# Attention values paired per head pair, converting loads of q and k, and output sums added by transfers: a fused attention and two-FFN kernel on one core

## The chip, the cores and the metric

The kernel runs on one core of one Trainium2 chip. A core has a matrix engine (TensorE, PE in the profile; its weight loads are PEld), three other compute engines (VectorE DVE, ScalarE ACT, GpSimd POOL) and a sync engine (SP). Each engine works through its own instruction list in order and waits on semaphores. Transfers are issued from the lists of SP, ACT and POOL and are carried by 16 DMA engines. The metric is device time in microseconds (us): the kernel before takes 1067.9 us, the median of three runs (1066.99, 1067.9 and 1069.63).

## The reference, cut to what matters

```
# attention: 4 batches, 8 heads, 576 positions, 64 columns a head
scores = (q @ k.T) / sqrt(64);  bias = -(cum_i - cum_j), cum = cumsum(relu(s))
p = softmax(where(causal, -1e9, scores + min(bias, 0)))     # divided by sum + 1e-9
x = p @ v                                                    # to 2304 tokens x 512
# first FFN, 512 -> 2048 -> 512
h = x @ w_in;  g = h if h >= 1, 0 if h <= -1, else (h + 1)^2 / 4;  y1 = g @ w_out
# second FFN, 512 -> 1536 -> 512
y2 = ((y1 @ w_a) * (y1 @ w_b)) @ w_out2
```

## The kernel before, in words

Everything is kept transposed, features on partitions and tokens along the free dimension. A batch has 576 tokens, which the FFN products take in two halves of 288 columns. For accuracy most products are split: a value is stored as a high word rounded to the format fp32r and a low word that holds the rest, and three products (high x high, high x low, low x high) are summed in PSUM. Products of plain fp32 operands need no split.

**Attention.** Query positions are cut in five tiles of 116 rows (the last has 112). For the 8 heads of batch 0 (QK32 = 8) the scores are plain fp32 products (line 644) on the raw q and k with the bias as extra rows. For batches 1 to 3 the scores (line 653) are two fp32r products on a tile `qk` of four planes: planes 0 and 1 hold the high words of q and k on both partition halves, planes 2 and 3 hold the high word of q again and the low words. `load_head` brings q and k into `qkraw` twice (four transfers from SP), ScalarE or GpSimd rounds them into `qk` (`qkhi`, `q1`, lines 374 and 378) and VectorE makes the low words (`qklo`, line 614). There are two `qkraw` and two `qk` tiles, so a head's load waits for the scores of the head two before it. VectorE adds the mask and takes the row maximum (line 672), ScalarE exponentiates (line 687), TensorE transposes the probabilities (line 712), and ScalarE, or VectorE in batch 0, copies them to SBUF as `pt`.

**Values.** `values` multiplies `pt` with v for one head and one of two regions of query columns (0 to 231, 232 to 575). A head has only 64 columns of v, half the array, so a region is cut at MID (146 and 430): its left piece is computed by the left 64 array columns and its right piece by the right 64, with the same v as weights. PV32 = 32 means that all 32 heads take this fp32 form. Two copies by ScalarE put the two pieces in place in `xraw`, which holds a pair of heads. The pair is scaled by the reciprocal sums (over PE in batch 0, over a round trip through DRAM in the other batches) and split in two words.

**FFN.** Batches 0 and 1 use plain split products (line 981). Batches 2 and 3 use a form of Strassen's method with seven products instead of eight for the first product of each layer (line 1128), with prepared forms of activations and weights. `y_step` makes the second product of a layer for a group of 3, 4 or 8 feature tiles: the first group is copied from PSUM to a tile y (ScalarE), each later one is added to it by VectorE (line 1223), and in layer 2 the finished tile is sent to the output by SP.

**Order.** The order on every engine is not the order of the code. A planner in the kernel (`Plan.run`) holds all operations with a key (a due time) and estimated costs, and places them engine by engine: of the first 24 in key order that have their buffers it takes the one that can start first. The keys come from the table ATT (start, end of each batch's attention), ENDS, LEAD (how long before use weights are fetched), AHEAD and OFFSET (within the seven products), and POOL_UNTIL (until which key GpSimd may take casts). On the chip an instruction waits for its semaphores only; the keys fix nothing but the order in each list.

Of the kernel before, what the change touches and what calls it, by code (L numbers as in the profile page):

```python
# [10 lines left out]
F32 = mybir.dt.float32  # L11
# [6 lines left out]
P = 128  # L18
# [8 lines left out]
ATT = ((0, 10, 60, False), (1, 65, 97, False), (2, 165, 350, True), (3, 340, 500, True))  # L27
# [8 lines left out]
ENDS = 1050  # L36
POOL_UNTIL = 100


OFFSET = (0.0, 0.15, 0.3, 0.45, 0.8, 0.95, 1.1)  # L40
AHEAD = 10
QK32 = 8
PV32 = 32
# [246 lines left out]
def tile_forgetting_attention_two_ffn(  # L290
# [35 lines left out]
    MID = (146, 430)  # L326
    REG_ALL = [len(j) * w for j, w in zip(REG_J, REG_W)]
    NG2 = NC // 2
    PE1 = 0.000456
    PE4 = 0.00168  # L330

# [77 lines left out]
    vs_room = room("vs", 1, [P, NQ, 2, D], F32R, "att")  # L409
# [4 lines left out]
    pt_rooms = [room(f"pt{g}_", 2, [QT, n], F32R, "att") for g, n in enumerate(REG_ALL)]  # L414
# [3 lines left out]
    hs_room = room("hs", 1, [P, S - PVSPLIT], F32, "att")  # L418
# [167 lines left out]
    def load_head(b, h, key):  # L586
# [14 lines left out]
        for u in range(2):  # L601
            for w in range(2):
                dma(key, lambda u=u, w=w: raw.t[u * D : (u + 1) * D, w], lambda w=w: qk[bh, :, w], D * S * 4, (),
                    [(raw, (u, w))], "qk", issue=0.6)
# [3 lines left out]
        op(casts(2 * S, key), key + 1,  # L608
           lambda e: copy(e, t.t[:, 0:2], raw.t), [(raw, (u, w)) for u in range(2) for w in range(2)],
           [(t, "hi"), (t, "lo")], name="qkhi")  # L610
        op(casts(S, key), key + 1, lambda e: copy(e, t.t[D:, 2], raw.t[D:, 0]), [(raw, (1, 0))] + ones_set, [(t, "q1")], name="q1")

# [3 lines left out]
           [(raw, (1, 0)), (raw, (1, 1)), (t, "hi")], [(t, "lo")], name="qklo", port=True)  # L616
        load_v(b, h, st, key)

    def load_v(b, h, st, key):
        vr = st["v"] = Ref(v_room, key)  # L620
        dma(key + 0.5, lambda: vr.t, lambda: v[b * H + h], P * NQ * D * 4, (), [(vr, 0)], "v")
        if b * H + h >= PV32:
            vs = st["vs"] = Ref(vs_room, key)
            op(casts(NQ * D, key), key + 1, lambda e: copy(e, vs.t[:, :, 0], vr.t), [(vr, 0)], [(vs, 0)], name="vhi")
            op({DVE: tt(NQ * D)}, key + 1,
               lambda e: nc.vector.tensor_tensor(vs.t[:, :, 1], vr.t, f32(vs.t[:, :, 0]), op=ALU.subtract),
               [(vr, 0), (vs, 0)], [(vs, 1)], name="vlo", port=True)

    def scores(b, h, i, key):
# [31 lines left out]
        need = [(t, j) for j in ("hi", "lo", "q1", ("bias", 0), ("bias", 1))] + ones_set  # L661
# [31 lines left out]
    def transposes(b, h, i, key):  # L693
# [7 lines left out]
        def part(t, kr, js):  # L701
            return t[:kr, js[0] * w : (js[-1] + 1) * w].rearrange(
                "k (j q) -> k j q", q=w
            )[:, :, q0 : q0 + r]

        for j0 in range(0, i + 1, 4):
# [12 lines left out]
            hi = st["pt"][0][g]  # L719
# [9 lines left out]
            if b * H + h >= PV32:  # L729
                lo = st["pt"][1][g]  # L730
                op({DVE: tt(n)}, key,
                   lambda e, src=src, js=js, kr=kr, lo=lo: nc.vector.tensor_tensor(
                       part(lo.t, kr, js), src(), f32(part(hi.t, kr, js)), op=ALU.subtract),
                   [(pt, 0), (hi, (i, j0))], [(lo, (i, j0))], name="ptlo")

    def values(b, h, g, key):
        st = heads[b, h]
        e = h % 2
        x = st["x"]
        a0, b0 = e * D, (1 - e) * D  # L740
# [3 lines left out]
        pts = [t[g] for t in st["pt"]]  # L744
        vt = st["v"] if b * H + h < PV32 else st["vs"]
        w = hi - lo
        need = [(t, (i, j0)) for t in pts for i in range(NQ) if (QT * i >= PVSPLIT) == (g == 1) for j0 in range(0, i + 1, 4)]
        need += [(vt, 0)] if b * H + h < PV32 else [(vt, 0), (vt, 1)]
        if b * H + h < PV32:


            mid = MID[g]
            ends = ((0, lo, mid), (D, mid, hi))

            def mm2(_):
                for j in js:
                    o = j * REG_W[g] - lo
                    for c0, l, u in ends:
                        q0 = max(l, QT * j)
                        if q0 >= u:  # L760
                            continue
                        nc.tensor.matmul(  # L762
                            ps.t[c0 : c0 + D, q0 - l : u - l],
                            vt.t[: rows[j], j],
                            pts[0].t[: rows[j], o + q0 : o + u],
                            start=(j == 0),
                            stop=(QT * (j + 1) >= u),
                        )

            cols = max(sum(max(0, u - max(l, QT * j)) for j in js) for _, l, u in ends)  # L770
            op({PE: cols * PE4 + 0.15}, key, mm2, need, [(ps, 0)], hold=[x], name="pv")
            for n, (c0, l, u) in enumerate(ends):
                op({ACT: act(u - l)}, key + 0.001 * n,
                   lambda e, c0=c0, l=l, u=u: copy(e, x.t[a0 : a0 + D, l:u], ps.t[c0 : c0 + D, : u - l]),
                   [(ps, 0)], [(x, (h % 2, g, n))], name="pvx")
            return
# [571 lines left out]
```

## Time and profile before

| what | value |
|---|---|
| median of three runs | 1067.9 us (1066.99 to 1069.63) |
| span of the profiled execution, first to last instruction | 1066.3 us |
| TensorE busy | 1047.7 us, 98% of the span |
| VectorE, ScalarE, GpSimd busy | 748.9, 612.8, 43.7 us |
| mean granted TensorE clock | 0.993 |
| transfers | 152.34 MB, mean 143 GB/s |

The time of the profiled execution is told by its span; the median of the runs is 1.6 us longer than that span. A time in a view counts from the span's start. "Busy" is the time in which an engine had at least one instruction under way. TensorE's matmuls overlap, so the time that one of them takes out of the engine's list is read from the difference of two starts, not from its own duration.

### The profile page before, as it was taken

The page shows a single profiled execution, that of the slowest core. Times are in us where ns is not written, and L with a number is a line of the kernel's source. Part 1 is how long each engine was busy: PE and PEld are TensorE (multiplying, and loading weights), DVE is VectorE, ACT ScalarE, POOL GpSimd, SP SyncE. Part 2 cuts the span into 40 slices and gives each one's busy share as a digit, 9 for nine tenths or more (in the row PEclk, how much of TensorE's full clock was granted, in tenths as well). Part 3 has the DMA queues.
Part 4 walks back from the last instruction along what each step waited for, and adds up shares of the span by engine and source line. Part 5 has one row for each costly group of instructions (what it writes and reads, how often), then busy time and mean ns, then how long its engine had stood idle before and what let it go on. Part 6 is the DMA issues. An engine that isn't in the chain of part 4 may idle for free.

```text
span 1066.3 us, 20668 instructions
## 1 busy us (share of the span) xinstructions
PE 1047.7 (98%) x8080; PEld 1003.4 (94%) x8080; DVE 748.9 (70%) x1471; ACT 612.8 (57%) x1332; POOL 43.7 (4%) x69
## 2 busy tenths in 40 slices
PE   9989998999999999999999999999999999999998
PEld 5769988999999999989999999999999999999998
DVE  6889867377787786657856677838576887378473
ACT  5878885666777876865775343645536543332130
POOL 2122320000000000000000000000000000000000
PEclk9999998999999999999999999999999999999999
DMA  5466639564564455545624464431313332231102
GB/s 174 158 209 201 210 118 276 185 224 143 176 215 157 149 198 188 183 139 163 209 87 147 168 229 173 150 101 58 119 40 120 96 103 80 80 99 61 41 1 89
DMA packets 71041, 152.34 MB, mean 143 GB/s; under 512 B 7592, under 2 KB 32168, under 8 KB 70944
## 3 DMA queue, kind: packets, MB, share of 16 engines
q1 hardware_dynamic: 70848, 150.88, 43.0%
q8 instruction: 63, 1.03, 0.4%
q14 instruction: 34, 0.28, 0.1%
q10 hardware_dynamic: 96, 0.15, 0.0%
HBM read 107.64 MB, written 42.79 MB: 141 GB/s over the span
## 4 chain that ended last, share of the span: by engine, by line
PE 92%; ACT 2%; DMA 2%; DVE 1%; issue 1%; SPq 1%; POOL 1%; ACTq 0%; DVEq 0%; POOLq 0%
PE pp L981 53%; PE pp L1128 12%; PE ps L1128 9%; PE ps L762 5%; PE ps L712 4%; PE ps L981 4%; PE ps L653 2%; PE ps L644 1%; PE pp L653 1%; DMA qkraw<-in_qk 1%; PE pp L644 1%; SPq L386 1%; DMA set<-keep_in 1%; ACT qk L374 1%; DMA conv<-in_w_in 1%
## 5 line engine op out<-in xcount | busy, mean ns | idle before, releaser
L981 PE MATMUL pp<-g,whl 128*128 128x288 f32 x2376 | 327.5, 296 | 0.0
L981 PEld LDWEIGHTS pp<-g,whl 128*128 128x128 f32 x2376 | 319.6, 189 | 0.8
L981 PE MATMUL pp<-x,whl 128*128 128x288 f32 x1896 | 270.4, 299 | 0.8 <-DVE early L1017 0.7
L981 PEld LDWEIGHTS pp<-x,whl 128*128 128x128 f32 x1896 | 256.9, 190 | 3.5 <-DVE early L1017 1.3
L1128 PE MATMUL pp<-form,set 128*128 128x288 f32 x960 | 149.0, 298 | 1.5 <-DVE ct L1147 1.5
L1128 PEld LDWEIGHTS pp<-form,set 128*128 128x128 f32 x960 | 133.6, 188 | 3.1 <-DVE ct L1147 2.0
L1128 PE MATMUL ps<-form,set 128*128 128x288 f32 x720 | 113.4, 296 | 0.7 <-DVE form L1099 0.7
L1223 DVE TENSOR_TENSOR y<-pp,y 128x576 f32<-128x576 f32 x76 | 57.4, 756 | 67.1 <-PE pp L981 66.7
L1128 PEld LDWEIGHTS ps<-form,set 128*128 128x128 f32 x720 | 101.6, 188 | 0.9 <-DVE form L1099 0.9
L687 ACT ACTIVATE p<-p,mx 112x576 f32<-112x576 f32 (+4 forms) x140 | 81.5, 583 | 7.5 <-DVE mx L672 6.6
L374 ACT COPY pt<-ps 112x112 f32<-112x112 f32 (+4 forms) x172 | 64.1, 391 | 21.1 <-PE ps L712 17.7
L1147 DVE TENSOR_TENSOR ct<-ps,ct 128x288 f32<-128x288 f32 x80 | 36.4, 455 | 51.5 <-PE ps L1128 39.4
L672 DVE CUSTOM_DVE_ANT_0 p<-ps,hide 116x116 f32<-116x116 f32 (+1 forms) x112 | 49.9, 453 | 29.2 <-PE ps L653 23.5
L942 ACT ACTIVATE conv<-conv 128x512 uint32<-128x512 uint32 x68 | 45.9, 675 | 41.5 <-DVE conv L952 28.0
L712 PE MATMUL ps<-ident,p 116*116 116x116 f32 (+2 forms) x420 | 62.5, 265 | 2.5 <-ACT pt L374 2.0
L762 PEld LDWEIGHTS ps<-pt,v 116*64 116x64 f32 (+1 forms) x832 | 51.4, 136 | 14.3 <-issue 7.8
L962 DVE TENSOR_TENSOR whl<-conv,whl 128x512 fp32r<-128x512 f32 x68 | 47.0, 697 | 25.3 <-ACT whl L374 24.6
L762 PE MATMUL ps<-pt,v 116*64 116x146 f32 (+5 forms) x832 | 62.6, 285 | 0.5 <-ACT pt L374 0.4
L374 ACT CAST whl<-conv 128x512 fp32r<-128x512 f32 x58 | 35.5, 617 | 38.5 <-PE pp L981 37.3
L712 PEld LDWEIGHTS ps<-ident,p 116*116 116x116 f32 (+2 forms) x420 | 46.0, 135 | 8.6 <-ACT pt L374 3.0
L1169 ACT CAST g<-ct 128x576 fp32r<-128x576 f32 x56 | 36.7, 675 | 29.3 <-PE pp L981 17.5
L653 PE MATMUL ps<-qk 128*116 128x116 f32 (+1 forms) x192 | 46.7, 337 | 5.8 <-DVE qk L614 4.0
(112 smaller groups left out, 1325.4 us busy)
## 6 DMA issues: line engine op xcount, KB each, us to landing
whl<-keep_out SPq DMA_DIRECT2D x36, 512.0 KB
qkraw<-in_qk SPq DMA_DIRECT2D x112, 144.0 KB
conv<-in_w_out SPq DMA_DIRECT2D x28, 512.0 KB
keep_out<-whl SPq DMA_DIRECT2D x28, 512.0 KB
conv<-in_w_in SPq DMA_DIRECT2D x16, 512.0 KB
keep_in<-whl SPq DMA_DIRECT2D x16, 512.0 KB
conv<-in_w_a SPq DMA_DIRECT2D x12, 512.0 KB
conv<-in_w_b SPq DMA_DIRECT2D x12, 512.0 KB
```

The lines of the kernel that those rows point to most:

```text
L374: nc.scalar.copy(o, i)
L653: nc.tensor.matmul(pv()[:r, a, :w], t.t[:, 2 * u, QT * i : n], t.t[:, 2 * u + 1, a * w : (a + 1) * w], start=(u == 0), stop=(u == 1),)
L672: nc.vector.tensor_tensor_reduce(out=psl(pref.t)[:r].rearrange("q (g n) -> q g n", g=parts), in0=pv()[:r, :parts, :w], in1=hide[:r, lag : ...
L687: nc.scalar.activation(p, p, AF.Exp, bias=mx.t[:r], scale=-1.0, accum_out=sm.t[:r, h % 2, i : i + 1])
L712: nc.tensor.transpose(pt.t[: rows[j], (j - j0) * QT : (j - j0) * QT + r], psl(pref.t)[:r, QT * j : QT * j + rows[j]], ident[:r, :r],)
L762: nc.tensor.matmul(ps.t[c0 : c0 + D, q0 - l : u - l], vt.t[: rows[j], j], pts[0].t[: rows[j], o + q0 : o + u], start=(j == 0), stop=(QT * ...
L942: op({ACT: act(512)}, k, lambda e: nc.scalar.activation(up(), low(), AF.Copy, scale=2.0**-29), [(wide, 0)], [(we, 0)], name="wlow")
L962: op({DVE: tt(512)}, k + 1, lambda e: vec.tensor_tensor(half(1), value(), f32(half(0)), op=ALU.subtract), [(wr, 0), (hl, 0)], [(hl, 1)], n ...
L981: nc.tensor.matmul(bank_of(ps, a)[:, :HN], w(wu), x(xu)[:, a * HN : (a + 1) * HN], start=(k == 0 and t == 0), stop=(k == len(terms) - 1 an ...
L1128: nc.tensor.matmul(at(to), by_pair(st.t)[:, w, wu, g], forms[b, layer, g].t[:, x, xu], start=fresh and k == 0, stop=k == len(terms) - 1, s ...
L1169: op({ACT: act(S)}, k, lambda e, f=f: nc.scalar.copy(g[f].t[:, 0], t.t[:, f]), need[f], [(g[f], 0)], name="ghi")
L1223: nc.vector.tensor_tensor(o, i, o, op=ALU.add)
```

## The change: what it does

1. **Values of a head pair.** `values` now works on two heads at once: the even head's product goes to the left 64 array columns and the odd head's to the right 64, over the whole region. It runs after the odd head's probabilities. One copy moves the whole 128-partition result to `xraw`. The cut MID and the split form are gone; `pt` needs less room, since the fifth key tile has only 112 query columns.
2. **High words by converting transfers.** `load_head` of batches 1 to 3 issues five transfers from GpSimd's list that read q and k from DRAM and write rounded words straight to `qk`: four for planes 0 and 1 on both halves (`qkhi`), one for the second copy of q (`q1`). The casts on ScalarE and GpSimd go. SP still loads q and k once to the upper half of `qkraw` for the low words.
3. **Layer 2's output sums by adding transfers.** Every group of layer 2 is copied from PSUM to y by ScalarE or VectorE. The first group goes to the output by SP; each later one by a transfer from GpSimd's list that adds to what is in DRAM. There are 40 adding transfers. Layer 1 is as before.
4. **New keys.** ATT, ENDS, LEAD, POOL_UNTIL, OFFSET and AHEAD have new values, which with the new costs gives a new order on all engines.

```diff
-ATT = ((0, 10, 60, False), (1, 65, 97, False), (2, 165, 350, True), (3, 340, 500, True))
+ATT = ((0, 12.083, 59.239, False), (1, 54.172, 107.501, False), (2, 110.043, 361.002, True), (3, 337.937, 539.099, True))
...
+PV2 = 0.00143
...
 # load_head, batches 1 to 3
-        for u in range(2):
-            for w in range(2):
-                dma(key, lambda u=u, w=w: raw.t[u * D : (u + 1) * D, w], lambda w=w: qk[bh, :, w], ...
+        for w in range(2):
+            dma(key, lambda w=w: raw.t[D:, w], lambda w=w: qk[bh, :, w], D * S * 4, (), [(raw, (1, w))], "qk", issue=0.6)
+            for u in range(2):
+                op({POOL: 1.0}, key, lambda e, u=u, w=w: nc.gpsimd.dma_start(t.t[u * D : (u + 1) * D, w], qk[bh, :, w]), (),
+                   [(t, ("hi", u, w))], move=D * S * 4, name="qkhi", lat=2.5)
+        op({POOL: 1.0}, key, lambda e: nc.gpsimd.dma_start(t.t[D:, 2], qk[bh, :, 0]), ones_set,
+           [(t, "q1")], move=D * S * 4, name="q1", lat=2.5)
...
-        op(casts(2 * S, key), key + 1,
-           lambda e: copy(e, t.t[:, 0:2], raw.t), ... name="qkhi")
-        op(casts(S, key), key + 1, lambda e: copy(e, t.t[D:, 2], raw.t[D:, 0]), ... name="q1")
...
+    def place(g, j):
+        lo = REG[g][0]
+        return j * REG_W[g] - lo if j < 4 else 3 * REG_W[g] - QT * j
 # values
         def mm(_):
             for j in js:
                 q0 = max(lo, QT * j)
+                for e, st in enumerate(pair):
+                    o = place(g, j)
                     nc.tensor.matmul(
+                        ps.t[e * D : (e + 1) * D, q0 - lo : hi - lo],
+                        st["v"].t[: rows[j], j],
+                        st["pt"][g].t[: rows[j], o + q0 : o + hi],
+                        start=(j == 0),
+                        stop=(j == js[-1]),
                     )
+        op({ACT: act(hi - lo)}, key, lambda e: nc.scalar.copy(x.t[:, lo:hi], ps.t[:, : hi - lo]),
+           [(ps, 0)], [(x, g)], name="pvx")
...
 # y_step
+        if layer == 2:
...
+            op({ACT: act(S), DVE: tt(S)}, k, move, both, [(y, e)], name="y0")
+            if first:
+                dma(key, lambda: to, ye, P * S * 4, [(y, e)], [("out", b, e)], "out")
+            else:
+                op({POOL: 1.0}, key, lambda _: nc.gpsimd.dma_start(to, ye(), accum_op=ALU.add),
+                   [(y, e)], [("out", b, e)], move=P * S * 4, name="out", lat=2.5)
+            return
```

**Three places in the order.** The first is TensorE's list, region 1 of head 0 in the kernel before (`ps` is a PSUM bank, `pt1_0` the head's transposed probabilities, `v0` its values; 64x198 is 64 array columns by 198 query columns):

```order
L762 MATMUL ps1_83<-pt1_0_322,v0_191 64x198
L762 MATMUL ps1_83<-pt1_0_322,v0_191 64x146
L762 MATMUL ps1_83<-pt1_0_322,v0_191 64x198
L762 MATMUL ps1_83<-pt1_0_322,v0_191 64x146
L762 MATMUL ps1_83<-pt1_0_322,v0_191 64x198
L762 MATMUL ps1_83<-pt1_0_322,v0_191 64x146
L762 MATMUL ps1_83<-pt1_0_322,v0_191 64x82
L762 MATMUL ps1_83<-pt1_0_322,v0_191 64x146
L762 MATMUL ps1_83<-pt1_0_322,v0_191 64x112
```

and the same region for heads 0 and 1 together in the changed kernel (`pt1_1` and `v1` are head 1's):

```order
L741 MATMUL ps2_84<-pt1_0_323,v0_191 64x344
L741 MATMUL ps2_84<-pt1_1_391,v1_210 64x344
L741 MATMUL ps2_84<-pt1_0_323,v0_191 64x344
L741 MATMUL ps2_84<-pt1_1_391,v1_210 64x344
L741 MATMUL ps2_84<-pt1_0_323,v0_191 64x344
L741 MATMUL ps2_84<-pt1_1_391,v1_210 64x344
L741 MATMUL ps2_84<-pt1_0_323,v0_191 64x228
L741 MATMUL ps2_84<-pt1_1_391,v1_210 64x228
L741 MATMUL ps2_84<-pt1_0_323,v0_191 64x112
L741 MATMUL ps2_84<-pt1_1_391,v1_210 64x112
```

Nine products a head have become ten a pair; neighbours in the list still use opposite halves of the array, now with two heads' weights. The whole list goes from 416 to 224 value products, and all other products keep their number.

The second place is GpSimd's list from its last setup steps on (`sm` are tiles of row sums, `whl` a weight tile), first before:

```order
L869 MEMSET sm0_246 116x10
L869 MEMSET sm1_254 116x10
L869 MEMSET sm2_256 116x10
L378 CAST whl0_293<-conv_73 128x2x256
L378 CAST whl1_395<-conv_73 128x2x256
L813 COPY over0_450<-sm0_246 116x640
```

and in the changed kernel (`qk0` and `qk1` are the tiles of heads 8 and 9):

```order
L823 MEMSET sm0_246 116x10
L823 MEMSET sm1_254 116x10
L823 MEMSET sm2_256 116x10
L602 DMA qk0_76<-in_qk 64x576 x4
L602 DMA qk1_77<-in_qk 64x576
L604 DMA qk0_76<-in_qk 64x576
L602 DMA qk1_77<-in_qk 64x576 x2
L378 CAST whl0_344<-conv_73 128x2x256
L602 DMA qk1_77<-in_qk 64x576
L604 DMA qk1_77<-in_qk 64x576
L767 COPY over0_414<-sm0_246 116x640
```

Eight converting loads for heads 8 and 9, which are due far later, now stand right behind the setup steps and ahead of the first weight cast; their tiles are free, so nothing but GpSimd's own pace holds them.

The third place is the end. Before, VectorE's last rows add to the four last y tiles (`y0_1` to `y3_1`, with the one before):

```order
L1223 TENSOR_TENSOR y3_0_10228<-pp1_81,y3_0_10228 128x576
L1223 TENSOR_TENSOR y0_1_10262<-pp0_80,y0_1_10262 128x576
L1223 TENSOR_TENSOR y1_1_10293<-pp1_81,y1_1_10293 128x576
L1223 TENSOR_TENSOR y2_1_10321<-pp0_80,y2_1_10321 128x576
L1223 TENSOR_TENSOR y3_1_10347<-pp1_81,y3_1_10347 128x576
```

In the changed kernel ScalarE's last rows copy the same tiles out of PSUM, and GpSimd's last five rows are the adding transfers of these tiles, in the same order:

```order
L374 COPY y3_0_9942<-pp0_80 128x576
L374 COPY y0_1_10026<-pp1_81 128x576
L374 COPY y1_1_10059<-pp0_80 128x576
L374 COPY y2_1_10087<-pp1_81 128x576
L374 COPY y3_1_10114<-pp0_80 128x576
```

The add has moved from VectorE behind the last product into the transfer, and that transfer from SP's list to GpSimd's.

## Rows read from the trace of the kernel before

**Rows 1.** The page: span, busy time of each engine, the chain by engine.
```profile
span 1066.3 us, 20668 instructions
...
PE 1047.7 (98%) x8080; PEld 1003.4 (94%) x8080; DVE 748.9 (70%) x1471; ACT 612.8 (57%) x1332; POOL 43.7 (4%) x69
...
PE 92%; ACT 2%; DMA 2%; DVE 1%; issue 1%; SPq 1%; POOL 1%; ACTq 0%; DVEq 0%; POOLq 0%
```

**Rows 2.** Windows: length; busy us (count) of PE PEld DVE ACT POOL; clock; DMA share; GB/s.
```profile
0.00:60.00 60.00, 58.34 (x397) 39.33 (x398) 46.67 (x135) 42.72 (x128) 13.33 (x29) 1.00 0.53 164
60.00:180.00 120.00, 111.81 (x919) 100.93 (x914) 98.69 (x221) 97.79 (x255) 29.79 (x35) 0.96 0.66 202
180.00:600.00 420.00, 417.24 (x3330) 405.05 (x3329) 286.91 (x567) 283.52 (x614) 0.54 (x5) 1.00 0.53 174
600.00:1066.00 466.00, 460.26 (x3443) 458.04 (x3442) 316.68 (x550) 188.78 (x336) 0.00 (x0) 1.00 0.29 97
```

**Rows 3.** Timeline of TensorE: start, duration, line, operation, instructions; scores, then values.
```profile
16.36 1.14 PE L644 MATMUL pp<-qkraw 68*112 68x288 f32 x4
17.33 0.66 PE L712 MATMUL ps<-ident,p 116*116 116x116 f32 x5
...
311.90 0.55 PE L762 MATMUL ps<-pt,v 116*64 116x146 f32 x8
312.38 0.61 PE L712 MATMUL ps<-ident,p 116*116 116x116 f32 x4
...
320.82 1.41 PE L762 MATMUL ps<-pt,v 116*64 116x198 f32 x18
322.15 3.44 PE L981 MATMUL pp<-g,whl 128*128 128x288 f32 x24
```

**Rows 4.** Who TensorE waited for: total, times, longest.
```profile
PE ps L653 <- DVE qk L614: 4.0, 1, 4.0
```

**Rows 5.** Windows at the two batch changes.
```profile
66.00:82.00 16.00, 12.89 (x93) 10.15 (x90) 13.74 (x29) 12.79 (x30) 4.26 (x6) 0.90 0.81 239
158.00:166.00 8.00, 4.03 (x39) 3.63 (x37) 6.82 (x12) 7.84 (x16) 2.05 (x2) 0.89 0.41 138
164.20:171.00 6.80, 4.92 (x20) 4.82 (x21) 6.74 (x15) 5.85 (x11) 2.52 (x2) 0.50 1.01 282
```

**Rows 6.** Chain in order of time (start, length, what), the two batch changes.
```profile
72.61 4.03 DMA qkraw<-in_qk
76.78 1.19 POOL qk L378
...
161.28 1.15 ACT qk L374
164.58 1.36 DVE qk L614
```

**Rows 7.** Windows of the start.
```profile
7.00:9.00 2.00, 2.00 (x10) 0.86 (x9) 1.18 (x2) 0.67 (x1) 0.00 (x0) 1.00 0.81 242
9.00:11.00 2.00, 2.00 (x11) 0.89 (x10) 0.00 (x0) 0.01 (x1) 0.00 (x0) 1.00 0.85 290
11.00:13.00 2.00, 2.00 (x11) 0.88 (x9) 0.72 (x2) 1.58 (x3) 0.00 (x0) 1.00 0.11 28
```

**Rows 8.** VectorE's timeline: the first row maximum of the scores.
```profile
15.05 0.27 DVE L672 CUSTOM_DVE_ANT_0 p<-ps,hide 116x116 f32<-116x116 f32 x1
```

**Rows 9.** Transfers of q and k: issue time from SP, minimum/median/maximum ns.
```profile
L386 SPq DMA_DIRECT2D qkraw<-in_qk x112: 465/584/1111, 1.7 to 483.6; - x112
```

**Rows 10.** Groups by line: count, busy us, mean ns of one.
```profile
L946 DVE TENSOR_SCALAR conv<-conv 128x512 f32<-128x512 f32 x68 | 29.1, 431 | 14.1 <-ACT conv L944 13.5
L950 DVE SCALAR_TENSOR_TENSOR conv<-conv 128x512 uint32<-128x512 uint32 x68 | 47.3, 696 | 1.2
L374 ACT COPY y<-pp 128x576 f32<-128x576 f32 x30 | 19.1, 637 | 35.2 <-PE pp L981 33.8 <-PE ps L653 1.4
```

**Rows 11.** Timeline of the end.
```profile
1062.49 0.76 DVE L1223 TENSOR_TENSOR y<-pp,y 128x576 f32<-128x576 f32 x1 [2.43 <-PE pp L981]
```

More of the change, by code (lines that the diff above doesn't have):

```diff
@@ L35 @@
 )
[L36 to L41, printed above, removed]
+ENDS = 1052
+LEAD = 14.238
+POOL_UNTIL = 110
+OFFSET = (0.0, 0.029, 0.184, 0.096, 0.755, 0.48, 1.1)
+AHEAD = 18
 QK32 = 8
-PV32 = 32
 OVER_PE = (0,)
@@ L325, in tile_forgetting_attention_two_ffn @@
     REG_W = [hi - lo for lo, hi in REG]
[L326 to L327 removed]
+    REG_ALL = [2 * REG_W[0], 4 * REG_W[1]]
     NG2 = NC // 2
@@ L728, in transposes, with values @@
                [(pt, 0)], [(hi, (i, j0))], name="pthi")
[L729 to L740, printed above, removed]
+    def place(g, j):
+        lo = REG[g][0]
+        return j * REG_W[g] - lo if j < 4 else 3 * REG_W[g] - QT * j
+    def values(b, pr, g, key):
+        pair = [heads[b, 2 * pr + e] for e in range(2)]
+        x = pair[0]["x"]
         lo, hi = REG[g]
@@ L743, in values @@
         ps = bank(key, "one")
[L744 to L776, printed above, removed]
-        cols = sum(hi - max(lo, QT * j) for j in js)
+        need = []
+        for st in pair:
+            need += [(st["pt"][g], (i, j0)) for i in range(NQ) if (QT * i >= PVSPLIT) == (g == 1) for j0 in range(0, i + 1, 4)]
+            need.append((st["v"], 0))
         def mm(_):
@@ L781, in mm @@
                 q0 = max(lo, QT * j)
[L782 to L783 removed]
+                for e, st in enumerate(pair):
+                    o = place(g, j)
                     nc.tensor.matmul(
[L785 to L798 removed]
+                        ps.t[e * D : (e + 1) * D, q0 - lo : hi - lo],
[3 more added lines that the diff above has]
+                        stop=(j == js[-1]),
+                    )
+        cols = sum(hi - max(lo, QT * j) for j in js)
+        op({PE: cols * PV2 + 0.15}, key, mm, need, [(ps, 0)], hold=[x], name="pv")
+        op({ACT: act(hi - lo)}, key, lambda e: nc.scalar.copy(x.t[:, lo:hi], ps.t[:, : hi - lo]),
+           [(ps, 0)], [(x, g)], name="pvx")
     def over_sums(b, pr, st, key, kx):
@@ L808, in over_sums @@
         parts = [(sm, (e, i)) for e in range(2) for i in range(NQ)]
-        x_all = [(x, (e, g, n)) for e in range(2) for g in range(2) for n in range(2)]
+        x_all = [(x, g) for g in range(2)]
         op({DVE: 0.45}, key, inv, (), parts, name="inv")
@@ L886, in attention @@
                 transposes(b, h, i, t + step * (0.6 + i / NQ))
-                if i == 1:
-                    values(b, h, 0, t + step * 1.1)
-            values(b, h, 1, t + step * 1.7)
+                if i == 1 and h % 2:
+                    values(b, h // 2, 0, t + step * 1.1)
             if h % 2:
+                values(b, h // 2, 1, t + step * 1.7)
                 c = h // 2
@@ L893, in attention @@
                 over_sums(b, c, st, t + step, kx)
-                x_all = [(x, (e, g, n)) for e in range(2) for g in range(2) for n in range(2)]
+                x_all = [(x, g) for g in range(2)]
                 if park:
@@ L1209, in ye, with move @@
             return y.t
-        last = final and layer == 2
+        if layer == 2:
+            def move(en):
+                for i, o in pieces(ps, ye()):
+                    copy(en, o, i)
+            to = out[sel, b * S : (b + 1) * S]
+            op({ACT: act(S), DVE: tt(S)}, k, move, both, [(y, e)], name="y0")
[5 more added lines that the diff above has]
+            return
         if first:
@@ L1225, in y_step @@
             op({DVE: tt(S)}, k, add, both, [(y, e)], name="yadd")
-        if last:
-            dma(key, lambda: out[sel, b * S : (b + 1) * S], ye, P * S * 4, [(y, e)], [("out", b, e)], "out")
-        elif final and (b, 1, 0) in forms:
+        if final and (b, 1, 0) in forms:
             if e % 2:
```

49 lines of the change are left out of this document (9 added, 40 removed).

## The prediction

> **What bounds the kernel now.** I read the page first: TensorE is busy 1047.7 of 1066.3 us and 92% of the chain that ended last is its own work [rows 1]. So a microsecond counts only if it leaves TensorE's list, or a wait of TensorE, or what lies behind its last product. The windows by stage come next [rows 2]. From 0 to 60 us TensorE idles 1.7 us, from 60 to 180 us 8.2 us with a mean clock of 0.96, from 180 to 600 us 2.8 us, and from 600 us on 5.7 us, of which the end takes 3.8 (1062.49 to 1066.3 [rows 1, 11]). Nearly all that can be won beside work itself lies between 60 and 180 us, where attention of batch 1 starts and ends. VectorE and ScalarE are busy 99 and 98 of those 120 us, and they are what TensorE waits for: the longest wait, 4.0 us, is for the low words of q and k, line 614 [rows 4]. I make the sum against the span of 1066.3 us; the median of the runs, 1067.9, is 1.6 us above it, which I carry over unchanged.
>
> **Values, costed from the timeline.** Region 0 of one head takes 312.38 - 311.90 = 0.48 us of TensorE's list, region 1 322.15 - 320.82 = 1.33 us [rows 3]. The two array halves stream side by side, so the longer column sum of the two pieces counts: 146 + 30 = 176 columns in region 0 (cut at 146), 3 x 146 + 146 + 112 = 696 in region 1 (right of the cut at 430). A line through both points has (1.33 - 0.48) / (696 - 176) = 1.635 ns a column and a fixed 0.19 us a burst. That rate has a check of its own: two plain fp32 score products of 288 columns (four records) take 17.33 - 16.36 = 0.97 us [rows 3], or 1.68 ns a column, so columns carry the cost and the 0.19 us belongs to the burst. After the change each half streams a whole head: 232 + 116 = 348 columns, 0.76 us; 3 x 344 + 228 + 112 = 1372 columns, 2.43 us. A pair costs 3.19 us where two heads cost 2 x 1.81 = 3.62. That is 0.43 x 16 = **6.9 us less**. The columns hardly change (1720 against 2 x 872); what halves is the number of bursts. From below: if the fixed part grew with the burst, only 24 columns a pair are won, 0.6 us in all. From above: if the fixed part sat in each product, two products a half in region 0 and five in region 1 would fit 0.195 us each and 0.5 ns a column, a pair would cost 2.2 us and 22 us would go; the score rows speak against that. I take 6.9.
>
> **Batch changes.** Between 66 and 82 us TensorE idles 3.1 us, and at a mean clock of 0.90 loses some 1.5 more [rows 5]. The chain there runs through a load of q and k of 4.03 us and a cast on GpSimd, and behind that the low words [rows 6]. Between 158 and 166 us it idles 4.0 us; right after, from 164.2 to 171, the granted clock is 0.50 (1.2 GHz), so of 4.9 busy us half is lost, 2.5 [rows 5]. The chain there is ScalarE's cast of q and k (1.15 us), other work of ScalarE and VectorE, then the low words (1.36 us) [rows 6]. Together 11.1 us. The change takes both casts out of these chains: high words of heads 8 and 9 are in place from the start, and only one load and line 614 remain. ScalarE's eight value copies a pair become two. What is late next is the load for the low words: SP issues head 8's behind the v loads of heads 6 and 7, which wait for the values of heads 4 and 5. From there four issues of 0.58 us [rows 9], about 3 us of flight and 1.36 us of line 614 make 6.7, against about 5 us of TensorE's list up to head 8's first score: 1736 columns of plain fp32 scores at 1.68 ns, 2.9 us, and 20 transposes, 2.6 us at most (five last 0.66 us and overlap [rows 3]). So some 2 us stay there, and I leave 1 for the second place: **8 us less**. From both sides: 11.1 less, or, if new waits of the same size take their place, none, or 4 more.
>
> **Start.** GpSimd is idle from 7 us [rows 7], so the eight converting loads that now stand behind its setup go out at once: 8 x 144 KB = 1.18 MB while the DMA engines are 0.81 to 0.85 busy at 242 to 290 GB/s [rows 7]. VectorE's first row maximum stands behind the steps of the first two weight tiles, at 15.05 us [rows 8], and these loads share the engines with exactly those tiles. If all 1.18 MB goes ahead, at 245 GB/s, the weights come 4.8 us later; if it queues behind, nothing is lost, since from 11 to 13 us the engines are 0.11 busy [rows 7]. I take **1.5 more**, a third, as SP has issued both weight loads before GpSimd is through its setup.
>
> **Converting loads in batch 1.** The `qk` tile is filled directly now, so a head's five loads cannot begin before the scores of the head two before it are done. In the changed list 73 records stand between that point and the first score of head 12, and 87 for head 10; at 111.81 / 919 = 0.122 us each [rows 2] that is 8.9 and 10.6 us of cover. Heads 13 to 15 have about 13 us, those of batches 2 and 3 over 15. The trace has no load from GpSimd. The nearest rows are SP's issue, 0.47 to 1.11 us [rows 9], flight within the 3.05 us behind VectorE's last add (1063.25 to 1066.3 [rows 1, 11]) or 4.03 us on busy engines [rows 6], and 1.36 us for line 614. That is 5 x 0.47 + 2.5 + 1.36 = 6.2 us to 5 x 1.11 + 4.03 + 1.36 = 10.9 us. I take issue at 1.0 and 3 us of flight, 9.4 us: head 12 is 0.5 us late, with hand-offs **1 more**; bounds 0 and 4 (2.0 and 0.3 us late, and a drop of the clock).
>
> The Trainium skill speaks against these loads. "SBUF — State Buffer", section "SBUF: two separate sides", warns that GpSimd cannot write a transfer's descriptors while VectorE runs an operation that holds their shared port pair, and its section "Who interferes with whom" counts tensor_scalar among those that can. Line 946 needs 431 ns for 512 columns and line 950, of the same size, 696 [rows 10], so such faster operations do run here. By that rule each of five issues may wait up to 0.43 us; head 12 would be 2.2 us later and the sum that much higher. No run so far has a load from GpSimd that would show it.
>
> **Layer 2 and the end.** Forty adds on VectorE (0.76 us [rows 11]) become copies (0.64 us on ScalarE [rows 10]) and transfers; both lie beside 24 products a tile, and ScalarE is busy 189 of the last 466 us [rows 2], so they cost nothing while TensorE works. Behind the last product the copy saves 0.12 us, and then an adding transfer takes the place of a plain one within the last 3.05 us. It reads its target before it writes it. Bounds: 0.1 less (same time) and 4 more (a flight like the 4.03 us [rows 6] once for reading, beside the write). I take **1 more**. "DMA: Bandwidth & Descriptors", section "Specifications", of the Trainium skill gives 1 us to the first byte from GpSimd's list and 0.6 from SP's; by that estimate alone this term would be 0.4, which no run here shows.
>
> **New keys elsewhere.** From 180 to 1062 us TensorE idles 4.7 us in all [rows 2, 11], so a new order can win little there and could lose as much: 0, with 4 on either side.
>
> **Sum.** -6.9 - 8 + 1.5 + 1 + 1 = -11.4, so 1066.3 becomes about 1054.9 and the median **1056.5 us**.
>
> **Rivals.** *Waits move, work goes.* The batch changes keep their 11.1 us in another form, for ScalarE's and VectorE's lists stay over 80% full there [rows 2]; only the values' 6.9 is won, and 3.5 is paid back at start, loads and end: 1067.9 - 6.9 + 3.5 = 1064.5. Against it: both chains lose an operation. *All stalls go.* The casts were the cause at both places, no load is late and the end costs nothing: 1067.9 - 6.9 - 11.1 - 1 = 1049. Against it: SP's v loads ahead of head 8's. *GpSimd's issue is slow* (this one ends slower). If an issue takes 2 us, held up by VectorE's steps or by the conversion itself, the chain is 5 x 2 + 3.5 + 1.4 = 14.9 us; heads 10 and 12 to 15 are late by 4.3, 6.0 and three times about 1.5, 15 us, each longer wait with a clock drop as in rows 5 (2.5 twice), the start costs its 4.8 and the end 4: 1067.9 - 6.9 - 8 + 15 + 5 + 4.8 + 4 = 1082. It decides from about 13 us of chain on, as then all heads of batch 1 wait. For it: GpSimd's loads stand in one list with casts; against it: no issue on SP takes over 1.11 us [rows 9]. The rule of the SBUF page named above is one way to it.
>
> **Chances.** Forecast (1051 to 1062) 0.60, waits move 0.20, all stalls go 0.12, slow issue 0.08. Within 0.3% means within 3.2 us, about what a measurement of this kernel can tell from no change. Faster by more than that: the forecast, all stalls go, and half of waits move, 0.81; within it 0.11; slower 0.08. The range that should hold the time 8 times in 10 is 1046 to 1066.
>
> **What would show it.** Value bursts of 0.76 and 2.43 us (start to next start); no cast between load and line 614; TensorE idle under 5 us from 60 to 180 us; the first row maximum at about 16.5 us; head 12's first score late by at most 1 us; the span ending some 4.8 us after the last product. It is wrong if a region-1 burst takes much less than 2.2 or as much as 2.7 us, if TensorE waits again at the change to batch 1 for over 5 us, or if it waits for loads of GpSimd at several heads.

## The result: 1.2% slower

The changed kernel takes 1080.11 us (median of 4 runs, 1079.27 to 1081.2), the kernel before 1068.37 beside it (4 runs). The ratio is 1.0119, 95% interval [1.0101, 1.0136]. Forecast was 1056.5, range 1046 to 1066, so even the sign was wrong. In three kernels below (e1, e10, e12) the runs of one kernel fall in two groups, told apart by their mean granted clock; the times of both are given.

The page after, span, busy time and granted clock in 40 slices, answers [rows 1]:
```profile
span 1079.4 us, 20016 instructions
...
PE 1050.9 (97%) x7696; PEld 990.4 (92%) x7696; DVE 721.5 (67%) x1428; ACT 581.2 (54%) x1248; POOL 125.2 (12%) x216
...
PEclk7699999999999999999999999999999999999999
```
TensorE has 384 records fewer (192 products, two records each) and is busy 3.2 us longer: its clock is 0.7 and 0.6 in the first two slices of 27 us, where it was 0.9 and more. The windows of [rows 2], after (columns as there), the first stretch cut finer below:
```profile
0.00:60.00 60.00, 55.98 (x244) 34.95 (x245) 33.16 (x95) 29.48 (x82) 15.58 (x35) 0.74 0.51 139
60.00:180.00 120.00, 111.77 (x811) 93.46 (x811) 99.67 (x238) 91.45 (x243) 37.26 (x66) 0.97 0.83 237
180.00:600.00 420.00, 415.62 (x3165) 398.72 (x3162) 281.76 (x563) 253.02 (x547) 50.77 (x91) 1.00 0.71 206
600.00:1066.00 466.00, 461.76 (x3443) 457.68 (x3442) 306.86 (x533) 205.86 (x375) 18.98 (x22) 1.00 0.38 108
...
4.20:14.40 10.20, 8.16 (x38) 3.53 (x36) 4.70 (x11) 2.56 (x4) 6.83 (x16) 1.00 1.12 265
14.40:45.10 30.70, 29.98 (x95) 19.95 (x97) 15.72 (x48) 14.32 (x42) 3.02 (x6) 0.50 0.35 101
45.10:60.00 14.90, 14.90 (x107) 10.44 (x104) 11.74 (x35) 11.32 (x35) 2.29 (x5) 1.00 0.43 134
```
For 30.7 us TensorE runs at 1.2 GHz while it is busy nearly all the time: half of that, 15 us, is lost in one place. The timelines of the start show what came before it (start, length, engine and line, operation, count, idle time ahead and what ended it). GpSimd's:
```profile
6.86 2.77 POOL L602 DMA_DIRECT2D qk<-in_qk  x5
9.57 0.57 POOL L604 DMA_DIRECT2D qk<-in_qk  x1
10.07 1.10 POOL L602 DMA_DIRECT2D qk<-in_qk  x2
```
TensorE's:
```profile
1.26 11.10 PE L494 MATMUL ps<-early 128*128 128x512 bf16 x44 [1.26 <-DVE early L489]
15.12 4.19 PE L634 MATMUL ps<-qkraw 68*116 68x116 f32 x8 [2.76 <-DMA qkraw<-g]
```
The eight converting loads go out from 6.9 to 11.2 us and fill the DMA engines (share 1.12 from 4.2 to 14.4 us). The small load that every first score needs, the bias rows (`qkraw<-g`), lands behind them, though SP issues it at the same time in both kernels. SP's timeline, after (the kernel before has the same line):
```profile
6.46 2.57 SPq L386 DMA_DIRECT2D qkraw<-g  x4
```
TensorE's 44 warm-up products (multiplications that compute nothing and only keep it busy until then) end at 12.4, TensorE idles 2.76 us, and the clock falls at 14.4, within the idle time.

The other places. TensorE's longest waits after (total, times, longest; [rows 4]):
```profile
PE ps L703 <- ACT p L677: 3.7, 2, 2.9
PE ps L930 <- ACT y L374: 3.5, 1, 3.5
PE pp L930 <- DVE early L966: 3.1, 3, 2.0
PE ps L634 <- DMA qkraw<-g: 2.8, 1, 2.8
```
The chain of work at the batch changes, after (start, length, what; [rows 6]):
```profile
159.02 6.19 DMA conv<-in_w_out
...
192.22 8.18 DMA qk<-in_qk
...
200.69 7.48 DMA qk<-in_qk
```
TensorE's timeline after, one burst of values in each region [rows 3] and the last products [rows 11]:
```profile
293.74 0.81 PE L741 MATMUL ps<-pt,v 116*64 116x232 f32 x8
294.48 0.48 PE L643 MATMUL ps<-qk 128*116 128x232 f32 x2
...
307.35 2.53 PE L741 MATMUL ps<-pt,v 116*64 116x344 f32 x20
309.82 1.45 PE L930 MATMUL pp<-g,whl 128*128 128x288 f32 x9
...
1068.72 3.09 PE L930 MATMUL pp<-g,whl 128*128 128x288 f32 x22
```
GpSimd's timeline after, the last adding transfer:
```profile
1072.77 0.86 POOL L1171 DMA_DIRECT2D out_y<-y  x1 [2.32 <-ACT y L374]
```
A pair's values take 0.74 + 2.47 us, start to next start. The casts are gone from the chains at the batch changes, but weight loads and converting loads of 6 to 8 us stand in them instead. The two converting loads shown, of heads 18 and 19 in batch 2, hold up an engine and not only their own scores. VectorE's line 610, which makes the low words, waits for them with other work behind it in VectorE's list (VectorE's timeline), TensorE waits for that work (TensorE's), and its clock falls once more (the window):
```profile
208.25 1.35 DVE L610 TENSOR_TENSOR qk<-qkraw,qk 64x1152 fp32r<-64x1152 f32 x1 [3.33 <-DMA qk<-in_qk]
```
```profile
211.12 8.14 PE L930 MATMUL pp<-x,whl 128*128 128x288 f32 x48 [2.04 <-DVE early L966]
```
```profile
212.40:215.80 3.40, 3.40 (x17) 3.40 (x16) 1.68 (x3) 1.31 (x2) 0.00 (x0) 0.50 0.47 156
```
From the last product (1071.81) to the end of the span it is 7.6 us, before 3.85.

### The profile page after: what moved, and what is told of

Its sections match the earlier page's. It is cut to its first block, busy times and chain, and to the rows that moved or that the text cites. A ratio compares the mean times of both kernels' runs of the same rounds, so it can differ in the third digit from the quotient of the medians.

```text
span 1079.4 us, 20016 instructions
## 1 busy us (share of the span) xinstructions
PE 1050.9 (97%) x7696; PEld 990.4 (92%) x7696; DVE 721.5 (67%) x1428; ACT 581.2 (54%) x1248; POOL 125.2 (12%) x216
## 3 DMA queue, kind: packets, MB, share of 16 engines
q0 software_dynamic: 15360, 29.50, 15.3%
## 4 chain that ended last, share of the span: by engine, by line
PE 68%; issue 9%; DMA 4%; POOL 1%; DVE 1%; ACT 1%; POOLq 0%; SPq 0%; DVEq 0%; ACTq 0%
PE pp L930 37%; PE pp L1077 12%; PE ps L1077 9%; PE ps L930 5%; DMA qk<-in_qk 3%; PE ps L741 2%; PE ps L703 2%; PE ps L643 1%; POOL out_y L1171 1%; PE pp L643 1%; DMA conv<-in_w_out 1%; POOL qk L602 1%; DMA g<-park 0%; ACT conv L893 0%; DVE form L1048 0%
## 5 line engine op out<-in xcount | busy, mean ns | idle before, releaser
L930 PE MATMUL pp<-g,whl 128*128 128x288 f32 x2292 | 317.8, 296 | 0.8 <-DVE y L376 0.6
L930 PEld LDWEIGHTS pp<-g,whl 128*128 128x128 f32 x2292 | 308.6, 188 | 2.1 <-DVE y L376 0.9
L1171 POOL DMA_DIRECT2D out_y<-y x40 | 34.9, 874 | 523.6 <-ACT y L374 473.1
L677 ACT ACTIVATE p<-p,mx 116x116 f32<-116x116 f32 (+4 forms) x140 | 81.7, 586 | 17.4 <-DVE mx L662 16.9
L374 ACT COPY pt<-ps 116x448 f32<-116x448 f32 (+5 forms) x179 | 67.1, 398 | 31.7 <-PE ps L703 31.1
L602 POOL DMA_DIRECT2D qk<-in_qk x96 | 49.8, 540 | 261.5 <-PE pp L643 233.4
L374 ACT COPY y<-pp 128x576 f32<-128x576 f32 x54 | 34.6, 641 | 78.2 <-PE pp L930 78.2
L741 PE MATMUL ps<-pt,v 116*64 116x344 f32 (+4 forms) x448 | 57.7, 397 | 0.7 <-DVE mx L662 0.7
L930 PE MATMUL ps<-g,whl 128*128 128x288 f32 x396 | 57.6, 295 | 0.0
L741 PEld LDWEIGHTS ps<-pt,v 116*64 116x64 f32 (+1 forms) x448 | 30.9, 143 | 26.7 <-issue 6.3
```

The costliest lines, as they stand in the source:

```text
L374: nc.scalar.copy(o, i)
L602: op({POOL: 1.0}, key, lambda e, u=u, w=w: nc.gpsimd.dma_start(t.t[u * D : (u + 1) * D, w], qk[bh, :, w]), (), [(t, ("hi", u, w))], move=D ...
L677: nc.scalar.activation(p, p, AF.Exp, bias=mx.t[:r], scale=-1.0, accum_out=sm.t[:r, h % 2, i : i + 1])
L741: nc.tensor.matmul(ps.t[e * D : (e + 1) * D, q0 - lo : hi - lo], st["v"].t[: rows[j], j], st["pt"][g].t[: rows[j], o + q0 : o + hi], start ...
L930: nc.tensor.matmul(bank_of(ps, a)[:, :HN], w(wu), x(xu)[:, a * HN : (a + 1) * HN], start=(k == 0 and t == 0), stop=(k == len(terms) - 1 an ...
L1171: op({POOL: 1.0}, key, lambda _: nc.gpsimd.dma_start(to, ye(), accum_op=ALU.add), [(y, e)], [("out", b, e)], move=P * S * 4, name="out", l ...
```

## The experiments

My theory: the early converting loads delay the bias rows, TensorE idles, the clock falls, and that is most of the loss. The rival: the new order, or the paired values, bring the clock down or make waits, and the loads are harmless. The time ranges that I wrote down held in e2, e6, e12, e14 and e15; e3 and e4 came out less than 0.5 us below theirs, and the others missed.

**e1_hold**: the changed kernel, with the ten converting loads of heads 8 and 9 issued only behind the first `spread` on GpSimd.
```
+ spread: ... while waiting: waiting.pop(0)()      # the ten held dma_start
```


> The changed kernel with the ten converting loads of heads 8 and 9 moved in GpSimd's list behind its first spread of reciprocal sums; all else in its order. Theory A (these loads delay the small load of the bias rows, TensorE idles 2.8 us before the first score, the granted clock falls to 0.50 and stays there for 30.7 us of the first scores): the idle and the half clock go, 1080.1 - 2.8 - 15.3 = about 1062 us, clock 1.00 through the first 60 us. Theory B (the clock falls because the new order of the first 60 us, with values paired, gives TensorE too little to do; the loads are harmless): the clock falls all the same, 1077 us or more.

1073.86 us, 10 runs: one at 1061.66 (clock 0.993), nine at 1071.3 to 1078.7 (0.981 to 0.986). The idle time at the start is gone and the clock holds there, but another idle time came. The ten loads are issued from 23.5 to 29 us; a weight load (`conv<-in_w_in`) that SP issues at 26.0 lands only at 33.1, ScalarE waits 2.06 us for it, and TensorE for ScalarE. The timelines of GpSimd and of ScalarE in e1:
```profile
23.47 3.02 POOL L612 DMA_DIRECT2D qk<-in_qk  x5
...
33.11 0.67 ACT L908 ACTIVATE conv<-conv 128x512 f32<-128x512 f32 x1 [2.06 <-DMA conv<-in_w_in]
```
TensorE's timeline, and the window that follows:
```profile
34.20 0.31 PE L713 MATMUL ps<-ident,g 116*116 116x116 f32 x1 [1.35 <-ACT g L687]
```
```profile
34.90:52.00 17.10, 16.93 (x60) 11.10 (x60) 8.27 (x23) 7.96 (x24) 2.06 (x4) 0.50 0.42 132
```
Behind 1.35 us of idle time come 17 us at 0.50. The 1062 us of theory A came in one run of ten; the traced run, one of the other nine, shows a way to miss it: the clock falls later, behind another late load.

**e2_warm**: the changed kernel with 14 more warm-up products, so that TensorE is busy until the bias rows land.
```
- for _ in range(4)
+ for _ in range(4 + 14 * (n == WARM - 1))
```


> The changed kernel with 14 more warm-up matmuls (0.216 us each, 3.0 us) behind the 44 that it has, so that TensorE is busy until the late bias rows land; the loads stay where they are. Theory A (the idle brings the clock down, and the clock costs five times what the late load costs): first score still near 15.2 us, clock 1.00 after it, 1080.1 - 15.3 = about 1065 us. Theory B (order or transfers bring the clock down): 1079 us or more. If the late load itself were the cost, 1080 as well.

1065.68 us (10 runs), ratio 0.9978 [0.9953, 1.0002]. The window from 0 to 60 us:
```profile
0.00:60.00 60.00, 58.07 (x339) 36.80 (x341) 43.06 (x129) 40.22 (x114) 18.16 (x39) 1.00 0.66 181
```
14 us come back for work that computes nothing, with all loads where they were. So the clock makes most of the loss at the start; how much is read below, beside e8.

**e3_gap**: the kernel before, with 14 of its 44 warm-up products left out.


> The kernel before with 14 of its 44 warm-up matmuls left out, so that TensorE idles some 3 us before the first score, which still comes at about 13.7 us; nothing else is changed and no load is added. Theory A: the clock falls to 0.50 and stays there for most of the first scores, 1068.4 + 13 to 16 = 1081 to 1084 us. Theory B: no change, 1068 us.

1080.56 us, ratio 1.0107 [1.0062, 1.0152]. TensorE's timeline and the window behind it:
```profile
12.46 1.41 PE L645 MATMUL ps<-qkraw 68*116 68x116 f32 x6 [3.09 <-DMA qkraw<-g]
```
```profile
14.50:45.20 30.70, 30.48 (x121) 21.75 (x123) 15.83 (x46) 15.16 (x47) 2.62 (x5) 0.50 0.33 100
```
No part of the change is in it, and idle time alone makes the loss, over 30.7 us as well. In this run the clock fell at 14.5 us, in a second idle time of 0.85 us behind the one of 3.09. It also shows when the bias rows land without the loads: 12.4 us.

**e4_loads**: the kernel before, with eight converting loads issued at the start.


> The kernel before with eight extra converting loads at the place in GpSimd's list where the changed kernel has them (into the same tiles, overwritten later by its own casts). Theory A: bias rows late by 1.5 us or more, TensorE idle before the first score, clock at 0.50 for some 25 to 30 us, 1068.4 + 15 to 18 = 1083 to 1086 us. Theory B: at most the lateness itself, 1068 to 1071 us.

1082.65 us, ratio 1.0111 [1.0077, 1.0146]. TensorE's first scores in the timeline:
```profile
16.34 4.18 PE L644 MATMUL ps<-qkraw 68*116 68x116 f32 x8 [3.20 <-DMA qkraw<-g]
```
The window behind it:
```profile
16.00:50.10 34.10, 33.77 (x133) 24.14 (x134) 16.64 (x48) 16.28 (x49) 2.92 (x5) 0.50 0.32 98
```
These loads alone turn the kernel before into one as slow as the changed one.

**e5_values, e6_values_keys, e7_no_adds, e8_no_loads**: the parts. e5 is the kernel before with paired values; e6 adds the new keys; e8 is the changed kernel with q and k loaded plainly and cast as before; e7 is e2_warm with layer 2's sums as before. The planner orders each of these kernels anew, so the number of a part holds its new order too.


> The kernel before with one part alone: the values of a head pair in one burst. Keys, loads of q and k and layer 2's sums are those of before. By my theory (the pair saves 0.43 us for each of 16 pairs and none of it is given back, the loss of the whole change lies in the loads, the end and the waits) 1061 us, 1059.5 to 1062.5, last product to span end 3.9 us as before. By the rival that a denser TensorE only meets its waits earlier, 1065 or more, with the waits of the batch changes longer by what the values saved.

> The paired values and the new keys; the loads of q and k and layer 2's sums are those of before. By my theory (the waits that the changed kernel shows at the batch changes come from converting loads that take 7 to 8 us there, not from the keys) 1057 to 1062, no clock at 0.50 in the first 60 us, and no wait over 2 us at 160 to 215 us. By the rival that the keys' order makes those waits, 1063 to 1068.

> The changed kernel with 14 more warm-up matmuls (1065.7 us so far) and layer 2's sums as before: vector adds, and the last sums sent by SyncE. By my theory the end gives back 3.7 us (last product to span end 3.9 for 7.6) and the wait of 3.5 us at 638 us stays, since a park load makes it: 1061 to 1063. If the copies on ScalarE made that wait, 1058 to 1060. By the rival that the adding transfers cost nothing, 1065 or more.

> The changed kernel with one part undone: high words of q and k by casts on ScalarE and GpSimd from plain loads, as before; paired values, new keys and adding transfers stay, and no warm-up is added. By my theory (the early converting loads hold the biases back, and TensorE's clock falls in the idle time) the clock stays at 1.00 in the first 60 us and the time is 1061 to 1066. By the rival (the new keys or the paired values make the idle time at the start) 1076 or more.

| kernel | us (runs) | ratio to before, 95% | last product to span end |
|---|---|---|---|
| e5: values | 1058.69 (4) | 0.9920 [0.9899, 0.9940] | 3.8 |
| e6: + keys | 1058.11 (4) | 0.9915 [0.9899, 0.9931] | 3.8 |
| e8: + adding transfers | 1058.87 (4) | 0.9924 [0.9906, 0.9941] | 7.9 |
| after: + converting loads | 1080.11 (4) | 1.0119 [1.0101, 1.0136] | 7.6 |
| e2: after + warm-up | 1065.68 (10) | 0.9978 [0.9953, 1.0002] | 7.6 |
| e7: e2 without adding transfers | 1064.53 (10) | 0.9975 [0.9960, 0.9989] | 4.0 |

The converting loads are 21 us, and everything else together gains 9. e8 came out below the range that I expected (1061 to 1066). e7 came out 1.2 us under e2, where I had expected some 3 to 5. The start of e8, TensorE's timeline and the windows:
```profile
12.67 1.41 PE L636 MATMUL ps<-qkraw 68*116 68x116 f32 x6
14.90 1.04 PE L636 MATMUL ps<-qkraw 68*116 68x464 f32 x2 [0.82 <-DVE mx L664]
```
```profile
0.00:60.00 60.00, 57.65 (x352) 36.96 (x352) 47.09 (x141) 42.02 (x117) 12.93 (x29) 1.00 0.58 172
60.00:180.00 120.00, 111.64 (x817) 97.43 (x817) 101.70 (x222) 89.88 (x231) 31.55 (x38) 0.97 0.72 226
```
No idle time ahead of the first score, clock 1.00. TensorE's region-1 burst of the third pair of batch 0, in e8, in e2 and in the changed kernel:
```profile
55.15 2.53 PE L743 MATMUL ps<-pt,v 116*64 116x344 f32 x20
...
58.29 2.54 PE L742 MATMUL ps<-pt,v 116*64 116x344 f32 x20
...
71.07 2.53 PE L741 MATMUL ps<-pt,v 116*64 116x344 f32 x20
```
Read at the end of such bursts, the changed kernel is behind e8 by 15.9 us at this pair (73.60 against 57.68), 17.3 at the last of batch 1 (182.08 against 164.75), and 21.2 at the last of all (623.79 against 602.57). So 16 us are lost at the start and 5.3 more on the way, 1.4 of them by the end of batch 1 and 3.9 behind it. Of the 16, e2 has 3.1 left (60.83; its first score comes at 16.06 where e8's comes at 12.67); the other 12.8 are the clock. In the profiled runs adding transfers bring the last product forward by 3.5 us (e8 1048.61, e6 1052.08; the wait at 610 to 620 us falls from 5.5 to 3.2) and give 4.1 back behind it.

**e9_adds_early**: e8, with adding transfers for batches 0 and 1 only.
```
- if layer == 2:
+ if layer == 2 and b < 2:
```


> The version without converting loads (1058.9 us: paired values, new keys, adding transfers), with the adding transfers kept for batches 0 and 1 only; batches 2 and 3 add on VectorE and send by SyncE. By my theory the adding transfers save 3.5 us of TensorE's time ahead of the layer change at 600 to 640 us and cost 4.1 us behind the last product, so that this version keeps the one without the other: 1054 to 1056, last product to span end 3.9 us. By the rival that the gain comes from the last round's lighter VectorE, 1058 to 1060.

1057.57 us (1056.17 to 1060.7), ratio 0.9906 [0.9884, 0.9929]; last product to end 3.9 us, but the wait for layer 2's copy is 4.2 us, 1 more than in e8. The best median, though e5, e6, e8 and e9 overlap: past the paired values nothing can be told from no gain.

**e10_first_loads, e11_later_loads**: e8 with the converting loads of heads 8 and 9 alone (`converts = bh < QK32 + 2`), or of heads 10 to 31 alone.


> The version without converting loads (1058.9 us), with the converting loads of heads 8 and 9 alone put back, eight of which are issued at the start. By my theory they cost what the changed kernel lost by the fifth burst of values, 16 us: 1073 to 1077, clock 0.50 for about 30 us. By the rival that the loads cost their time all along the attention, 1060 to 1066.

> The version without converting loads (1058.9 us), with the converting loads of heads 10 to 31 put back, so none at the start. By my theory the clock stays at 1.00 in the first 60 us and what is left is the longer waits at the batch changes, 2 to 6 us: 1061 to 1065. By the rival that later loads cost nothing (their landing is hidden), 1058 to 1060; by the rival that all of them cost alike, 1070 or more.

e10: 1070.79 us, in two groups: three of 10 runs at 1058.3 to 1059.6 (clock 0.993), seven at 1069.0 to 1075.7 (0.978 to 0.984). The profiled one is of the second; TensorE's timeline and the window:
```profile
14.42 2.87 PE L652 MATMUL ps<-qkraw 68*116 68x116 f32 x8 [1.39 <-DMA qkraw<-g]
```
```profile
16.00:43.50 27.50, 27.50 (x93) 17.97 (x93) 14.46 (x47) 13.96 (x42) 3.02 (x6) 0.51 0.35 108
```
That is below the 1073 to 1077 that I expected. The three runs are as fast as e8; the seven are 10 to 17 us slower. The three have no trace, so whether TensorE idled in them is not known.

e11: 1072.1 us (7 runs), far above my 1061 to 1065. Its start is clean; the loss lies at the end of batch 1. The window from 120 to 165 us (DMA share and GB/s stand last) in e8:
```profile
120.00:165.00 45.00, 40.34 (x285) 35.45 (x285) 39.95 (x82) 32.36 (x80) 11.09 (x14) 0.92 0.73 248
```
The same window in e11, TensorE's longest wait, and the chain there:
```profile
120.00:165.00 45.00, 33.68 (x238) 29.40 (x239) 36.02 (x78) 31.25 (x79) 13.95 (x26) 0.85 0.89 247
```
```profile
PE ps L721 <- ACT p L695: 9.9, 3, 7.6
```
```profile
143.58 6.86 DMA conv<-in_w_out
...
155.50 6.48 DMA conv<-in_w_in
```
ScalarE waits for weights twice, and TensorE for ScalarE. The engines are fuller at the same GB/s.

**e12_half_gap**: the kernel before with 7 warm-up products left out.


> The kernel before with 7 of its 44 warm-up matmuls taken out, so that TensorE idles about 1.5 us ahead of the first score (14 out left 3.25 us and cost 13 us). By my theory an idle time of this size in the first scores brings the clock down as well (one of 1.5 us at 33 us did): 1076 to 1083. If only the longer idle time does, 1066 to 1069.

1078.41 us: three of 10 runs at 1066.0 to 1068.2, seven at 1074.5 to 1080.9. In the traced run, one of the seven, the idle time came in two parts, 0.61 and 0.92 us, and the clock still fell; e8's 0.82 us by itself did not bring it down.

**e13_spare, e14_plain**: e8 plus five loads per head from 10 on, to a place in device memory that nothing reads; e13 converts, e14 does not.
```
+ op({POOL: 1.0}, key, lambda e, ...: nc.gpsimd.dma_start(spare[:, :S], qk[bh, :, w]), ...)
```


> The version without converting loads (1058.9 us), with five more converting loads by GpSimd for each head from 10 on, which go from device memory to a spare place in device memory that nothing reads; high words are still cast on ScalarE and GpSimd. By the theory that the loads cost through traffic (the weights' loads beside them land later, ScalarE's list waits behind these) 1064 to 1074, a DMA share of 0.85 or more at 120 to 165 us, and a wait at 140 to 165 us longer than in the version without. By the rival that it is the late landing of the high words, 1058 to 1061.

> As the run with spare converting loads, but the spare loads copy 4-byte words without converting. By the theory of traffic, bytes alone decide: within 2 us of the run with converting spare loads. By the rival that converting makes the DMA engines slow, at least 3 us less than that run, and a smaller DMA share at 120 to 165 us.

1076.23 and 1077.01 us. Loads that nobody waits for come with 17 us, so late high words are not needed for a loss; nor is converting, as plain copies cost as much. But the DMA share was 0.77, below my 0.85, and the planned order differs from e8's, so the 17 us are not the loads' alone. These loads also write to device memory and not to SBUF.

**e15_same_order**: the spare converting loads inside e8's own order, which is the same on every engine but GpSimd. **e16_last_loads**: e8 with real converting loads for heads 16 to 31.


> The version without converting loads (1058.9 us) in its own order on TensorE, ScalarE, VectorE and SyncE; beside each plain load of q or k of heads 10 to 31 GpSimd issues one converting load (for one of the four, two) to a spare place in device memory that nothing reads. By the theory that traffic and GpSimd's issuing cost the time at the batch changes 1062 to 1070. By the rival that the order made the 17 us of the runs with spare loads (their order was planned with the loads in it), 1058 to 1060.

> The version without converting loads (1058.9 us), with real converting loads for heads 16 to 31 (batches 2 and 3) alone. By the theory that the loads cost only where the DMA engines are near full and TensorE waits on loads (60 to 180 us), 1058 to 1060. By the rival that a converting load costs wherever it stands, 1064 or more.

e15: 1066.36 us (10 runs, 1065.54 to 1076.49), 7.5 above e8 by traffic and GpSimd's issuing alone; the rest of e13's 17 us goes with its order. The same load of q and k in the chain, first in e8, then in e15 (its traced run took 1071.2 us, 4.8 above its median):
```profile
64.67 3.16 DMA qkraw<-in_qk
```
```profile
68.24 5.79 DMA qkraw<-in_qk
```
e16: 1067.52 us, where I expected 1058 to 1060. Heads 16 and 17 load while batch 1 ends: from 140 to 160 us the DMA share is 0.99 where e8 has 0.67, TensorE is busy 10.6 us where it was 15.3; and behind the last product lie 10.8 us, 2.9 more (below). Yet at the last burst of values e16 is only 1.6 us behind e8 (604.19 against 602.57): little of what TensorE missed there is left (the orders of the two differ). 3.2 us more are lost at the change of layer, where TensorE waits 4.7 us instead of 3.2 for layer 2's copy and the mean clock from 604 to 640 us is 0.95. So this run does not show that the loads of batches 2 and 3 cost their time where they stand.

## Why the prediction was wrong, point by point

- **Values, -6.9: right.** 0.74 + 2.47 = 3.21 us a pair (forecast 0.76 + 2.43), 0.41 less than before, 6.6 in all; e5 measures 9.3 with an interval of 6.4 to 10.8, its new order included.
- **Start, +1.5 with bounds 0 to 4.8: the step that failed, some 16 us.** I asked when the weights come and priced lateness one for one. What came late was the bias rows, by 2.7 us (15.1 against 12.4), and 12.8 of the 16 us are not the lateness but the clock behind it: 30.7 us at 0.50. The sign of this was in my own rows: [rows 5] show 0.50 behind a wait of 4.0 us, which I used at the batch change and not at the start, where [rows 7] have no idle time. That the first row maximum came near the forecast (15.97, forecast 16.5) is luck: it waited for the first score and not for the weights.
- **Batch changes, -8: nothing came; the second step that failed.** TensorE idles 8.2 us between 60 and 180 us before and after (120 less 111.81 and 111.77), and 7.8 in e2, where the casts are gone too and the clock holds at the start; the mean clock there stays at 0.96 to 0.97. The casts left the chain and loads took their place: the rival *Waits move, work goes*, which I gave 0.20. With the start put at 16 and this term at 0, the same sum gives 1056.5 + 14.5 + 8 = 1079, near the 1080.1 measured.
- **Converting loads in batch 1, +1: 1.4 there and 3.9 behind it, by a mechanism of which I had half.** An issue takes 0.54 us (mean of line 602's group), not 1.0, but the loads of heads 18 and 19 took 6.9 to 8.3 us from issue to landing, where I had 3 of flight. I gave the heads of batch 2 over 15 us of cover, and TensorE did not wait for their scores. But line 610 stands in VectorE's list ahead of work that TensorE needs: it waited 3.33 us, and behind it TensorE waited 2.04 us and ran 3.4 us at half clock. Over the whole kernel line 610 waits 11.2 us, in eight places, for converting loads. The loads also slowed others: 3.16 us became 5.79 in e15. The Trainium skill, "DMA: Bandwidth & Descriptors", section "Issuing engines are not separate DMA queues", says that transfers started by any engine share the same 16 DMA engines and interleave; e15's pair of rows agrees (3.16 and 5.79 us). That VectorE holds up GpSimd's issuing, the rule weighed in the prediction, no run shows: the longest issue of line 602 is 0.70 us.
- **Layer 2 and the end, +1: 4.1 behind the last product, but 3.5 won ahead of it**, which I had put at nothing; together 0.8 (e8 less e6). Of the 4.1, some 1.5 lie behind the last byte: from there to the end of the span it is 2.8 us in e8 and 1.3 in e6.
- **New keys, 0 with 4 either way: right** (e6 less e5, -0.6).
- *GpSimd's issue is slow* (1082) was near the time by another way: no issue took its 2 us (line 602's took 0.51 to 0.70).

Not settled: how much of the 5.3 us is VectorE's wait for the loads, how much traffic and how much GpSimd's time, as no run has one of them alone; and why e11 and e13 lose more than the changed kernel does at the same place, where their orders differ.

## What to carry to other kernels

Ask of every added early transfer which small load of the first product queues behind it, and price an idle TensorE by how long the clock then stays low, not by its length. Before a load is called free because its own reader can wait, look at the DMA share of that stretch, at who else is waiting for a load there, and at what stands behind the reader in its engine's list. Time each part alone: here one part hid the gain of another.

## What the runs showed that I had not expected

TensorE's clock stayed at 0.50 for 27 to 34 us while TensorE was 97% busy or more with 4-byte products (e3, e4, e10, the changed kernel), behind idle times of 1.39 to 3.2 us. And a span can end well behind its last transfer where GpSimd issued that: in e16 the last product ends at 1053.4 and nothing moves from 1058.2 us on, yet the span ends at 1064.2 (a window of its end). From the last byte to the end of the span it is 2.8 us in e8 and 1.3 to 1.4 in the kernel before, e6 and e9, where SP sends the last sums; what the span waits for there no view shows.
```profile
1058.20:1064.20 6.00, 0.00 (x0) 0.00 (x0) 0.00 (x0) 0.00 (x0) 0.00 (x0) 0.50 0.00 0
```
